# A three-part fused kernel: spreading products moved behind a slot's last cosine step, one scale moved behind two conversions, bank copies moved ahead of the rounding of pieces

## The chip, the cores and the metric

The kernel runs on one core of one Trainium2 chip, in one launch. The metric is device time in microseconds (us) of that launch. The kernel before took 914.43 us, the median of three executions (906.65, 914.43 and 920.22).

The engines are named as the profile names them: PE (TensorE, matmuls; PEld is its loading of weights), DVE (VectorE), ACT (ScalarE), POOL (GpSimd) and SP (SyncE, which issues the DMAs).

## The reference

Three stages follow each other, all in float32. `q`, `k`, `v` have the shape (4, 8, 576, 64).

```python
attn_out = attention(q, k, v)          # softmax; heads 0-3 see a window of 32, heads 4-7 every 32nd position
x = attn_out.transpose(0, 2, 1, 3).reshape(2304, 512)

h = x @ moe_w_in                       # 512 -> 2048
x = (h * cos(h)) @ moe_w_out           # 2048 -> 512

g = x @ moe2_w_gate                    # 512 -> 1536
silu = g * (1.0 / (1.0 + exp(-g)))
out = (silu * (x @ moe2_w_val)) @ moe2_w_out   # 1536 -> 512
```

## The kernel before, in words

**Number format.** A float32 product is made of three float16 products: each operand is split into a high and a low float16 part (`hi_part` on ACT, L245; `lo_part` on DVE, L248), and `mm3` (L540 to L543) adds hi·hi, hi·lo and lo·hi. So that the parts stay in range, every matrix and every block of activations is first multiplied by a power of two. That scale needs the largest magnitude of the whole matrix, over all 128 partitions, and it comes in two steps:

- *tops*, `spread_tops` (L117 to L131): DVE reduces the column maxima to one per partition, keeps the exponent and writes it on the diagonal of a 128x128 tile, `tops`.
- the *spreading product*, `common_scale` (L133 to L138): PE multiplies a matrix of ones with that tile into a bank of PSUM (L136), so that every partition sees all 128 maxima, and DVE reduces them to `q` (L137) and derives the scale and its inverse (L112 to L114).

So a scale goes DVE, then PE, then DVE. On PE the product is one matmul of 128 columns, but PE takes its work in order, and so does DVE: until `tops` is written, everything behind the product on PE stands still, and until the product is done, everything behind `q` on DVE does.

**The first MLP** (about 112 to 519 us) runs over 5 blocks of tokens (512, 512, 512, 384, 384) and 16 strips of 128 hidden columns: 80 *slots*, numbered through. The order within a slot is written out in the loop at L1009 to L1046. In slot k

- PE makes the strip, `up1(k)`: 12 matmuls into one of four banks. Then it does `down1` for one or two older strips (12 matmuls each into the accumulators).
- ACT does `up1_a(k)` (L574, rounding of the phase) and, for an older strip, `finish` (L588, the high part of its result, whose low part POOL makes, L589); later `up1_c(k-1)` (the sine, L581).
- DVE does `up1_b(k-1)` (L577), then *first-half fill*, then `up1_d(k-2)` (L584, the last step of the cosine: it multiplies by the strip that is still in the bank, and by that frees the bank), then *second-half fill*.

The four banks are handed round: a strip's bank is free again when its `up1_d` has run. A spreading product takes a bank of the same four and gives it back when `q` has read it. DVE runs behind PE in this loop, in places by more than ten microseconds, and the banks limit by how much.

**Fill** is the conversion of the later weights (`w_out`, then `gate` and `val` of the second MLP, then `w_out2`): integer steps that make float32 out of the float64 words (ACT L224, DVE L231 and L235), sums on POOL (L894), hi and lo parts, and scans for the maximum (L174). It is a queue of steps with costs, and `pump` takes from it while a credit, fed by each slot in proportion to its PE time times `SHARE` or `SHARE2`, lasts. *Urgent* pieces (`scale_pieces`: four maxima L521, tops, spreading product; `split_pieces`; `fold_pieces`) prepare the activations of the next block; `pump_urgent` takes exactly one per slot, just behind `up1_b`. Both queues can hand out a spreading product in the first half, ahead of `up1_d`.

`open_weights` (L930) queues the second MLP's weights: gate's scale, six pairs of gate (each a `half_later`, with the scans of val beside it), tops of val, val's scale, six pairs of val.

**The second MLP** (about 519 us to the end) has 30 slots s, 6 per block, in the loop from L1160. A pair of strips of gate and val is made by seven products of half the size (`multiply`, numbers 0 to 6) into banks. Sums of banks are formed by copying one bank to SBUF (`snap`, ACT L1184) and adding it to another on DVE (`join`, L1188). Then come the tanh (`gate_tanh`, ACT L652), the two steps of the silu (DVE L658 and L659), and the splitting of the result and of sums of its quarters into pieces (`piece_hi`, ACT L663; `piece_lo`, DVE L666) which the down products (`downs`, L693) take. The silu of a slot's second half, its sums and the pieces of it (`second_set`, `third_set`) are done at the start of the next slot, beside that slot's products.

## Time and profile before

| | |
|---|---|
| runs | 906.65, 914.43, 920.22 us; median 914.43 |
| the profiled execution | 906.64 us, of which 904.6 us are the span from first to last instruction |
| PE busy | 858.6 us (95%) |
| DVE busy | 688.8 us (76%) |
| ACT busy | 522.0 us (58%) |
| POOL busy | 200.0 us (22%) |
| mean granted clock of PE | 0.983 of full |
| chain that ended last | PE 68%, DVE 13%, ACT 6%, issue 5%, DMA 5%, POOL 2% |

Busy time is a share of the whole span, over parts that are limited by different engines. A wait of PE is shown behind the instruction that waited, in brackets: how long PE had been idle, and which instruction's end let it go. The window view gives the busy microseconds of each engine in a stretch, with the number of instructions, the granted clock of PE as a share of full speed, and the DMA's share.

### The profile page before, as it was taken

The numbers are of one execution on the slowest core, as the hardware profiler recorded it, in microseconds if no ns is written. First come the engines' busy times: TensorE is split into PE (matmuls) and PEld (weight loads), VectorE is DVE, ScalarE is ACT, GpSimd is POOL, SyncE is SP. The second block draws the span as 40 slices with busy tenths as digits, with TensorE's granted clock in tenths as the row PEclk, the third lists the DMA queues.
The fourth block names the chain that finished last, engine by engine and source line by source line (L and its number), as shares of the span: only waits on it lengthen the run. The fifth ranks groups of instructions, "written<-read, shape, count | busy, mean of one in ns | idle before, by whom it ended". The sixth has DMA issues, their size and how long they took to land.

```text
span 904.6 us, 18561 instructions
## 1 busy us (share of the span) xinstructions
PE 858.6 (95%) x7228; PEld 606.8 (67%) x7228; DVE 688.8 (76%) x1337; ACT 522.0 (58%) x1046; POOL 200.0 (22%) x253
## 2 busy tenths in 40 slices
PE   7999999989985989989999988999999999999998
PEld 4766644434432434445656676888888899999998
DVE  4898899894998697857977488867885776776672
ACT  4889978653665566547778455545445444544440
POOL 3444224121554365223222300000000000000000
PEclk7899999999998989999999999999999999999999
DMA  9998841565697265702514623867677688888894
GB/s 300 354 305 259 275 139 47 175 214 197 233 312 253 93 226 174 283 27 76 184 65 179 249 91 154 310 204 271 230 264 260 214 272 288 294 292 310 317 326 153
DMA packets 55912, 200.61 MB, mean 222 GB/s; under 512 B 5552, under 2 KB 19376, under 8 KB 51984
## 3 DMA queue, kind: packets, MB, share of 16 engines
q1 hardware_dynamic: 55824, 199.42, 64.6%
q8 instruction: 57, 0.93, 0.4%
q14 instruction: 31, 0.25, 0.1%
HBM read 175.41 MB, written 23.99 MB: 220 GB/s over the span
## 4 chain that ended last, share of the span: by engine, by line
PE 68%; DVE 13%; ACT 6%; issue 5%; DMA 5%; POOL 2%; SPq 0%; ACTq 0%; POOLq 0%; DVEq 0%
PE acc L693 14%; PE bank L541 11%; PE bank L542 10%; PE bank L543 10%; PE acc L541 6%; PE acc L543 6%; PE acc L542 6%; DMA vl<-v_l 3%; DVE arena L248 2%; PE bank L435 2%; PE po L488 2%; DMA v_pair<-v_s 1%; DVE tb L577 1%; DVE cv L235 1%; DVE tb L584 1%
## 5 line engine op out<-in xcount | busy, mean ns | idle before, releaser
L541 PE MATMUL bank<-xs,wi 128*128 128x256 f16 (+3 forms) x780 | 234.3, 300 | 18.3 <-DVE q L137 8.3
L542 PE MATMUL bank<-xs,wi 128*128 128x256 f16 (+3 forms) x780 | 234.3, 300 | 0.0
L543 PE MATMUL bank<-xs,wi 128*128 128x256 f16 (+3 forms) x780 | 234.1, 300 | 0.0
L589 POOL TENSOR_TENSOR arena<-tb,arena 128x512 f16<-128x512 f32 (+1 forms) x80 | 92.7, 1160 | 251.5 <-ACT arena L588 225.7
L542 PEld LDWEIGHTS <-wi 128*128 128x128 f16 x880 | 86.3, 98 | 58.5 <-issue 26.3
L541 PEld LDWEIGHTS <-wi 128*128 128x128 f16 x880 | 86.3, 98 | 46.3 <-issue 12.2
L541 PE MATMUL acc<-arena 128*128 128x512 f16 (+1 forms) x320 | 114.6, 358 | 0.0
L542 PE MATMUL acc<-arena 128*128 128x512 f16 (+1 forms) x320 | 114.5, 358 | 0.0
L543 PE MATMUL acc<-arena 128*128 128x512 f16 (+1 forms) x320 | 114.5, 358 | 0.0
L543 PEld LDWEIGHTS <-wi 128*128 128x128 f16 x880 | 86.4, 98 | 35.9 <-issue 1.9
L693 PEld LDWEIGHTS <-arena 128*128 128x128 f16 x1080 | 100.8, 98 | 8.1
L678 POOL TENSOR_TENSOR wi<-tb 128x256 f32<-128x256 f32 (+1 forms) x30 | 20.2, 672 | 347.2 <-DVE tb L659 347.2
L663 ACT ACTIVATE arena<-tb 128x256 f16<-128x256 f32 (+3 forms) x59 | 28.9, 489 | 114.0 <-DVE tb L659 109.0
L542 PEld LDWEIGHTS <-arena 128*128 128x128 f16 x600 | 58.7, 98 | 38.1 <-issue 5.6
L693 PE MATMUL acc<-arena 128*128 128x256 f16 (+1 forms) x702 | 82.0, 265 | 0.0
L543 PEld LDWEIGHTS <-arena 128*128 128x128 f16 x600 | 58.7, 98 | 32.8
L541 PEld LDWEIGHTS <-arena 128*128 128x128 f16 x600 | 58.8, 98 | 32.7 <-issue 0.3
L574 ACT ACTIVATE tb<-bank,quarter,c 128x512 int32<-128x512 f32 (+1 forms) x75 | 54.3, 723 | 41.3 <-PE bank L543 28.6
L658 DVE SCALAR_TENSOR_TENSOR tb<-tb,arena 128x512 f32<-128x512 f32 (+1 forms) x60 | 38.0, 633 | 45.0 <-ACT tb L652 45.0
L588 ACT ACTIVATE arena<-tb 128x512 f16<-128x512 f32 (+1 forms) x80 | 46.5, 582 | 39.5 <-PE acc L543 37.2
L541 PE MATMUL bank<-xs,arena 128*128 128x256 f16 (+1 forms) x240 | 62.8, 262 | 4.4 <-ACT cv L1184 3.8
L543 PE MATMUL bank<-xs,arena 128*128 128x256 f16 (+1 forms) x240 | 62.9, 262 | 0.0
(146 smaller groups left out, 1723.5 us busy)
## 6 DMA issues: line engine op xcount, KB each, us to landing
wi<-w SPq DMA_DIRECT2D x20, 1792.0 KB, 8.7
arena<-w SPq DMA_DIRECT2D x60, 576.0 KB, 4.4
raw<-w_out SPq DMA_DIRECT2D x56, 512.0 KB, 4.8
arena<-w SPq DMA_DIRECT2D x10, 1792.0 KB, 14.9
raw<-w_gate SPq DMA_DIRECT2D x24, 512.0 KB, 4.3
raw<-w_val SPq DMA_DIRECT2D x24, 512.0 KB
w<-arena SPq DMA_DIRECT2D x36, 256.0 KB, 3.2
raw<-w_in SPq DMA_DIRECT2D x16, 512.0 KB
```

Of the source, the lines that this page charges most:

```text
L248: nc.vector.scalar_tensor_tensor(out=dst, in0=src, scalar=s, in1=hi, op0=ALU.mult, op1=ALU.subtract)
L435: nc.tensor.matmul(out=self.sc[r, i, :], lhsT=qk_t[self.i][r, q0:q0 + 64], rhs=qk_t[self.i][r, k0:k0 + w], start=i == 0, stop=False)
L541: nc.tensor.matmul(out=o, lhsT=w[:, 0, c], rhs=x[0], start=first, stop=False, **kw)
L542: nc.tensor.matmul(out=o, lhsT=w[:, 0, c], rhs=x[1], start=False, stop=False, **kw)
L543: nc.tensor.matmul(out=o, lhsT=w[:, 1, c], rhs=x[0], start=False, stop=last, **kw)
L574: nc.scalar.activation(out=c["w"].bitcast(I32), in_=c["ph"], func=AF.Identity, scale=turn[c["blk"]], bias=quarter)
L588: nc.scalar.activation(out=g[:, 0, 0:n], in_=w, func=AF.Copy)
L589: nc.gpsimd.tensor_tensor(out=g[:, 1, 0:n], in0=w, in1=g[:, 0, 0:n], op=ALU.subtract)
L658: nc.vector.scalar_tensor_tensor(out=t, in0=t, scalar=1.0, in1=gate, op0=ALU.add, op1=ALU.mult)
L663: nc.scalar.activation(out=to, in_=src, func=AF.Copy, scale=2.0 ** -11)
L678: nc.gpsimd.tensor_tensor(out=t_sums[:, 0, 0:h], in0=c["t"][0][:, h:2 * h], in1=c["t"][0][:, 0:h], op=ALU.subtract)
L693: nc.tensor.matmul(out=o[:, c], lhsT=w[:, 256 * i + 128 * c:256 * i + 128 * c + 128], rhs=unit(u)[:, x:x + h], start=j == c == i == 0, sto ...
```

## The change

Four edits. The number of instructions on each engine is the same as before, and the order of DMA issues is too.

1. Spreading products of `scale_later` (weights) and of `scale_pieces` (activations) are marked `late`. The first half of a slot's fill stops in front of one; `pump_urgent(False)` ahead of `up1_d` takes an urgent piece only if it isn't late, and `pump_urgent(True)` behind `up1_d` takes one only if it is. As both calls stand in every slot, tops and spreading product of an urgent chain now fall into one slot where they took two.
2. val's scale is queued behind the first two conversions of val's first pair (`ready`), where it stood directly behind tops.
3. In the second MLP `snap(px)` stands ahead of the last slot's tanh and silu, and the two halves of `second_set` stand behind the second and third snaps, just ahead of `third_set`.
4. `SHARE2` is 0.78 where it was 0.75 (blocks 2 to 4).

```diff
-SHARE, SHARE2, SB = 0.95, 0.75, 2
+SHARE, SHARE2, SB = 0.95, 0.78, 2
...
-        def pump(share):
+        late = set()
+
+        def pump(share, spread=True):
             credit[0] = min(credit[0] + share, max(share, 1.0))
-            while fill and credit[0] > 0:
+            while fill and credit[0] > 0 and (spread or fill[0][1] not in late):
                 step_fill()
...
         def scale_later(mat, bound):
-            later(0.6, lambda: scale_w.__setitem__(mat, common_scale(tops[mat], bound)))
+            def spread():
+                scale_w[mat] = common_scale(tops[mat], bound)
+            late.add(spread)
+            later(0.6, spread)
...
-            yield 0.6, lambda: scales.__setitem__(blk, common_scale(box["top"], TX))
+            def spread():
+                scales[blk] = common_scale(box["top"], TX)
+            late.add(spread)
+            yield 0.6, spread
...
-        def half_later(j, mi, mat, beside=None):
+        def half_later(j, mi, mat, beside=None, ready=None):
...
+            if ready:
+                begin([])
+                ready()
             parts = [[(0, lambda q=q: hi(q)), (0.7, lambda q=q: lo(q))] for q in range(3)]
...
                 top_later("val")
-                scale_later("val", TW_IN)
                 for j in range(NPR):
-                    half_later(j, 1, "val")
+                    half_later(j, 1, "val", ready=None if j else lambda: scale_later("val", TW_IN))
...
-        def pump_urgent():
-            if urgent:
+        def pump_urgent(now=None):
+            if urgent and (now is None or (urgent[0][1] in late) == now):
...
-                pump_urgent()
-                pump(budget * 0.5)
+                pump_urgent(False)
+                pump(budget * 0.5, False)
                 up1_c(steps[-1][2])
                 if len(steps) > 1:
                     up1_d(steps[-2][2])
+                pump_urgent(True)
                 pump(budget * 0.5)
...
+            a = snap(px)
             if last:
                 t = gate_tanh(last, 1)
                 silu(last, 1, t)
-            a = snap(px)
...
             if last:
                 piece_sums(last)
-                his, los = second_set(last)
-                run(his)
             pz = halves(bank(), h)
             multiply(4, w, x, pz, h, True)
             b = snap(pz)
...
-            if last:
-                run(los)
             pump_urgent()
             multiply(5, w, x, px, h, False)
             a = snap(px)
             if last:
+                his, los = second_set(last)
+                run(his)
+                run(los)
                 his, los = third_set(last)
                 run(his)
```

**DVE, slots 39 and 40 of the first MLP** (the scale of block 1's result for the second MLP; L577 is `up1_b`, L584 `up1_d`, L248, L231 and L235 are fill). Before, from the tops to the scale:

```order
L130 TENSOR_SCALAR tops<-id_76,p 128x128
L248 SCALAR_TENSOR_TENSOR arena<-arena,s_3646 128x512
L231 TENSOR_SCALAR arena<-arena 128x512
L235 SCALAR_TENSOR_TENSOR arena<-raw,arena 128x512
L584 SCALAR_TENSOR_TENSOR tb<-tb,bank 128x512
L248 SCALAR_TENSOR_TENSOR arena<-arena,s_3646 128x512 x2
L248 SCALAR_TENSOR_TENSOR arena<-arena,s_3646 128x256
L231 TENSOR_SCALAR arena<-arena 128x512
L235 SCALAR_TENSOR_TENSOR arena<-raw,arena 128x512
L577 SCALAR_TENSOR_TENSOR tb<-bank,c_3439,tb 128x512
L137 TENSOR_REDUCE q<-bank 128x1
L112 RECIPROCAL s_3982<-q 128x1
```

Now, one slot earlier (L586 is `up1_b`, L593 `up1_d`, L250 and L233 are L248 and L231):

```order
L130 TENSOR_SCALAR tops<-id_76,p 128x128
L250 SCALAR_TENSOR_TENSOR arena<-arena,s_3694 128x512
L250 SCALAR_TENSOR_TENSOR arena<-arena,s_3694 128x256
L593 SCALAR_TENSOR_TENSOR tb<-tb,bank 128x512
L137 TENSOR_REDUCE q<-bank 128x1
L112 RECIPROCAL s_3877<-q 128x1
L113 TENSOR_SCALAR inv_3878<-q 128x1
L114 TENSOR_SCALAR s_3877<-s_3877 128x1
L233 TENSOR_SCALAR arena<-arena 128x512
L237 SCALAR_TENSOR_TENSOR arena<-raw,arena 128x512
L586 SCALAR_TENSOR_TENSOR tb<-bank,c_3437,tb 128x512
```

`q` stood behind the next slot's `up1_b`; now it stands behind the `up1_d` of the slot that wrote tops, with two fill steps between tops and `up1_d`.

**DVE, slots 34 and 35** (tops and scale of val). Before:

```order
L130 TENSOR_SCALAR tops<-id_76,p 128x128
L137 TENSOR_REDUCE q<-bank 128x1
L112 RECIPROCAL s_3646<-q 128x1
L113 TENSOR_SCALAR inv_3647<-q 128x1
L114 TENSOR_SCALAR s_3646<-s_3646 128x1
L577 SCALAR_TENSOR_TENSOR tb<-bank,c_3439,tb 128x512
L521 TENSOR_REDUCE parts_3_3561<-xy_69 128x1
```

Now:

```order
L130 TENSOR_SCALAR tops<-id_76,p 128x128
L233 TENSOR_SCALAR arena<-arena 128x512
L586 SCALAR_TENSOR_TENSOR tb<-bank,c_3437,tb 128x512
L526 TENSOR_REDUCE parts_3_3570<-xy_69 128x1
L237 SCALAR_TENSOR_TENSOR arena<-raw,arena 128x512
L233 TENSOR_SCALAR arena<-arena 128x512
L593 SCALAR_TENSOR_TENSOR tb<-tb,bank 128x512
L237 SCALAR_TENSOR_TENSOR arena<-raw,arena 128x512
L137 TENSOR_REDUCE q<-bank 128x1
```

On PE val's product stood behind slot 34's down products, with that of `ys` just ahead of it; now it stands behind those of slot 35, and the two conversions of val's first pair (L233 and L237, twice) stand ahead of `q`.

**ACT, a slot of the second MLP** (L1242 is the last copy of the slot before). Before:

```order
L1242 ACTIVATE arena<-bank 128x2x256
L652 ACTIVATE tb<-arena,c_5641 128x512
L1184 ACTIVATE cv<-bank 128x512
L663 ACTIVATE arena<-tb 128x2x256
L1184 ACTIVATE cv<-bank 128x512 x2
L663 ACTIVATE arena<-wi 128x4x256
```

Now (L1253 is that copy, L1196 `snap`, L661 the tanh, L672 `piece_hi`):

```order
L1253 ACTIVATE arena<-bank 128x2x256
L1196 ACTIVATE cv<-bank 128x512
L661 ACTIVATE tb<-arena,c_5657 128x512
L1196 ACTIVATE cv<-bank 128x512 x2
L672 ACTIVATE arena<-tb 128x2x256
L672 ACTIVATE arena<-wi 128x4x256
```

The first copy goes ahead of the tanh, and the rounding of `second_set` from between the first and second copy to behind the third.

## Rows read from the trace of the kernel before

**Rows 1.** The page: busy time of the engines.

```profile
PE 858.6 (95%) x7228; PEld 606.8 (67%) x7228; DVE 688.8 (76%) x1337; ACT 522.0 (58%) x1046; POOL 200.0 (22%) x253
```

**Rows 2.** The waits view: engine, tile, line waited for: us, times, longest.

```profile
DVE q L137 <- PE bank L136: 19.9, 7, 5.8
...
PE bank L136 <- DVE tops L130: 10.0, 3, 8.7
PE bank L541 <- DVE q L137: 8.3, 7, 3.4
PE bank L541 <- DVE tb L584: 7.6, 6, 2.3
PE bank L541 <- ACT cv L1184: 5.3, 8, 1.5
```

**Rows 3.** Windows: us busy (instructions) of PE, PEld, DVE, ACT, POOL; clock, DMA, GB/s.

```profile
190.00:200.00 10.00, 8.49 (x40) 3.81 (x39) 9.48 (x19) 6.91 (x11) 2.50 (x3) 1.00 0.76 240
...
290.00:300.00 10.00, 7.06 (x26) 2.92 (x26) 4.54 (x14) 1.68 (x3) 0.00 (x0) 0.68 0.24 84
...
330.00:340.00 10.00, 5.96 (x18) 2.12 (x17) 9.61 (x19) 7.32 (x12) 6.80 (x7) 0.69 0.69 229
```

**Rows 4.** PE's timeline, slots 33 to 36: start, us, instruction, [idle before it].

```profile
270.50 0.38 PE L541 MATMUL bank<-xs,wi 128*128 128x512 f16 x1
270.72 0.38 PE L542 MATMUL bank<-xs,wi 128*128 128x512 f16 x1
...
292.94 0.27 PE L136 MATMUL bank<-tops,ones 128*128 128x128 bf16 x1 [8.73 <-DVE tops L130]
...
299.82 0.38 PE L541 MATMUL bank<-xs,wi 128*128 128x512 f16 x1
```

**Rows 5.** DVE's timeline, slots 32 to 36.

```profile
275.50 0.67 DVE L584 SCALAR_TENSOR_TENSOR tb<-tb,bank 128x512 f32<-128x512 f32 x1
...
292.63 0.25 DVE L130 TENSOR_SCALAR tops<-id,p 128x128 bf16<-128x128 bf16 x1
...
301.24 0.94 DVE L231 TENSOR_SCALAR arena<-arena 128x512 int32<-128x512 int32 x1 [6.20 <-ACT arena L224]
```

**Rows 6.** ACT's and POOL's timeline ahead of val's tops.

```profile
284.66 0.63 ACT L588 ACTIVATE arena<-tb 128x512 f16<-128x512 f32 x1
...
286.48 3.45 POOL L894 TENSOR_TENSOR arena<-arena 128x256 f32<-128x256 f32 x4
```

**Rows 7.** PE's and DVE's timeline, slots 38 to 41.

```profile
318.09 0.38 PE L541 MATMUL bank<-xs,wi 128*128 128x512 f16 x1
...
322.22 0.74 DVE L577 SCALAR_TENSOR_TENSOR tb<-bank,c,tb 128x512 f32<-128x512 f32 x1
...
324.00 0.68 DVE L584 SCALAR_TENSOR_TENSOR tb<-tb,bank 128x512 f32<-128x512 f32 x1
...
331.81 0.22 PE L136 MATMUL bank<-tops,ones 128*128 128x128 bf16 x1 [0.61 <-DVE tb L584]
335.46 0.58 PE L541 MATMUL bank<-xs,wi 128*128 128x512 f16 x1 [3.43 <-DVE q L137]
...
340.53 0.46 PE L541 MATMUL acc<-arena 128*128 128x512 f16 x1
```

**Rows 8.** PE's timeline, two later slots with a wait for a scale.

```profile
399.76 0.32 PE L541 MATMUL bank<-xs,wi 128*128 128x384 f16 x1 [1.97 <-DVE q L137]
...
464.36 0.32 PE L541 MATMUL bank<-xs,wi 128*128 128x384 f16 x1 [1.38 <-DVE q L137]
```

**Rows 9.** Windows of the second MLP, columns as in Rows 3.

```profile
540.00:550.00 10.00, 6.57 (x58) 5.44 (x56) 7.56 (x14) 5.10 (x10) 0.73 (x1) 1.00 0.51 185
...
590.00:600.00 10.00, 10.00 (x94) 8.97 (x92) 5.16 (x8) 3.81 (x7) 0.73 (x1) 1.00 0.53 151
```

**Rows 10.** ACT's timeline at the start of a slot of the second MLP.

```profile
543.83 0.72 ACT L652 ACTIVATE tb<-arena,c 128x512 f32<-128x512 f32 x1
...
546.04 0.63 ACT L663 ACTIVATE arena<-tb 128x512 f16<-128x512 f32 x1 [1.00 <-DVE tb L659]
```

## The prediction

> **What bounds the kernel now.** I read the page first: PE is busy for 95% of the span and DVE for 76% [rows 1], so as a whole it is bound by PE, and what a change can give is PE's idle time. The waits of PE come next [rows 2]: after the attention part few lines hold it up. A spreading product waits for its tops (10.0 us, of which one wait is 8.7), strips wait for a bank that `q` holds (8.3 in seven waits, the longest 3.4), for a bank that `up1_d` holds (7.6 in six), and products of the second MLP for a copied bank (5.3 in eight). DVE's own wait for spreading products (19.9 us in seven) counts only where PE ends up waiting behind it.
>
> Then the windows [rows 3], to see which engine sets the pace where these waits lie. In the first MLP between 190 and 340 us DVE is 9.5 to 9.6 of 10 us busy while PE has gaps: there DVE sets the pace and the ring of four banks passes it on to PE. From 590 us on PE is 10.00 of 10 us busy [rows 9], and nothing that the change does there can move the end. In the same windows the granted clock tells a second cost: 1.00 in 190 to 200 us, where the waits are of 2.3 us and less, but 0.68 and 0.69 around the 8.73 us wait and around the pair 0.61 and 3.43 us [rows 3, 4, 7]. It fell to its lower level (1.2 of 2.4 GHz) there and came back. From 335.46 to 340.53 one strip's 12 matmuls took 5.07 us [rows 7]; at full clock they start 0.216 us apart (two are shown rounded, 270.50 and 270.72 [rows 4]), so a strip of 512 tokens or a down product of one takes 2.6: 2.5 us lost. The other place, with nearly the same mean clock, I put at 2.0.
>
> **What goes.** `q` no longer stands in front of an `up1_d`, and its product has been on PE for two fill steps and that `up1_d` when DVE comes to it. So the seven waits on `q` can go: 3.43 [rows 7], 1.97 and 1.38 [rows 8], and four that share the remaining 1.52. With them go the 0.61 [rows 7], val's 8.73 [rows 4], the last scale's share of the tops waits (0.7 of 10.0, estimated as half of what lies beside the 8.73 in three waits), and both drops of the clock, 4.5. That is 8.3 + 0.6 + 8.7 + 0.7 + 4.5 = 22.8 us, 2.5% of the profiled 906.6, if nothing comes in their place.
>
> **What comes.** Before, PE met a spreading product a slot after DVE had been told to write its tops. Now both belong to one slot, so PE stands at the product until DVE, which is behind, comes to that slot's tops; and the next strip needs the bank of the `up1_d` that lies behind the first half of that slot's fill. Where DVE runs late this is a new stall. Three places:
>
> - *Slot 32* (scale of block 0's result). PE began strip 33 at 270.50 [rows 4]. Its bank now comes from the `up1_d` of slot 32, which DVE ended at 275.50 + 0.67 = 276.2 [rows 5]: 5.7 us later.
> - *Slot 35* (val). PE now does strip 35 and a down product (2.6 + 2.6 us) before it asks for the tops, so of 8.73 some 3.5 are left. But the tops hang on a chain from PE: ACT L588 behind slot 34's down products (284.66), POOL's sums (3.45 us), ACT's and DVE's parts, tops at 292.63 + 0.25, 8.7 us behind PE's last matmul at 284.2 [rows 4 to 6]. The stall in slot 32 shifts that start by about 4.7 us (5.7 less what the next strips waited for their banks). Tops then end near 297.6, PE is there at 294.4 (strip 33 from 276.2, its down product, then strips and down products of slots 34 and 35: 276.2 + 5.2 + 7.8 + 5.2), and strip 36 waits another 3 us for its `up1_d`. That is 300.5, and it was 299.82 [rows 4]. Val's gain is given back by the stall that slot 32 has got.
> - *Slot 38* (scale of block 1's result). PE began strip 39 at 318.09 [rows 7]. DVE came to that slot's `up1_b` at 322.22 and to its `up1_d` at 324.00; with the tops between them (0.25 for the last of three steps at 292.63 [rows 5], the other two put at as much each) `up1_d` ends near 324.68 + 0.75 = 325.4. Strip 39 begins 7.3 us later. Then slot 39 (2.6 + 5.2), slot 40 (2.6 + 2.6) and strip 41 (2.6) end at 341.0 at full clock; strip 41 ended at 340.53 before [rows 7].
>
> So this stretch comes out 0.5 us later at full clock. Two things move it. DVE had idled 6.20 us at 301.24, for val's first conversions, which stood behind the scale and behind ACT [rows 5]; these conversions now stand ahead of the scale, so DVE can gain 0 to 6.2, and I take 2, nearer to nothing, as PE and ACT bring what it works on. And the clock: the three new stalls are about 6, 6 and 7 us in two parts each, and resemble the pair that halved it (0.61 and 3.43). Between none and three drops of 2.5 us the cost is 0 to 7.5; since DVE, not PE, sets the pace there and a slow strip is hidden behind its lag, I take 2. Term: +0.5 − 2 + 2 = **+0.5**.
>
> The Trainium skill, in "TensorE: Matmul & The Clock Gate", section "HAM oscillation — how this bites in real kernels", says that waits between bursts of matmuls drop the clock, so that the next burst starts cold, each time. The trace agrees for the two long waits (clock 0.68 and 0.69) and shows none for the short ones (1.00 in 190 to 200 us). Taken strictly, all three new stalls pay.
>
> *Blocks of 384 tokens* (slots 48 to 79): 1.97, 1.38, two of the four small waits (0.8) and the 0.7 go, 4.9 in all. Three spreading products with their tops in the same slot come (slots 54, 64 and 77). DVE is less far behind here; each costs between 0 and 3.4 (the longest wait on `q`), I take 1.4, near what these slots show now [rows 8]. Term: −4.9 + 4.2 = **−0.7**.
>
> *The second MLP.* The first copy goes ahead of a tanh of 0.72, the second ahead of a rounding of 0.63 [rows 10]; the eight waits of 5.3 us [rows 2] lie in the first ten slots, where PE is 6.6 of 10 us busy in the worst window [rows 9]. All could go: −5.3. But the circle from tanh over silu, join and the last copy back to tanh sets the pace in these slots, and a copy, put at the 0.63 of the rounding, is now part of it: in slots 1 to 5 that is up to 5 × 0.63 = +3.1. Pieces come later for the downs, which from 590 us have slack. I take −1.5, between the two and somewhat on the side of the shown waits. Term: **−1.5**.
>
> *Slot 9 and `SHARE2`*: the early product may meet its tops late (0 to 1.3 by the two smaller waits on tops); DVE limits the slots that follow, so 0. A share of 0.78 moves fill earlier and adds no instruction: 0, with its ends within those of the first term. No DMA issue changes place, so SP's queue and POOL's order stay.
>
> **Sum:** +0.5 − 0.7 − 1.5 = −1.7 us on the profiled 906.6 (904.6 of span and 2.0 around it), which is also the fastest of the three runs. The median lies 7.8 above it; the forecast is set against the median: 914.4 − 1.7, **913**.
>
> **Rivals.**
>
> - *A, the waits change places* (forecast): 905 to 921, taking the ends of the terms but not all at once, and 4 us for a median of three runs that lie 13.6 apart. Chance 0.62.
> - *B, what comes is cheap.* DVE uses its idle 6.2 us fully, is then less far behind when PE reaches slots 35 and 38, and the clock does not fall. For it: DVE's idle time lies just ahead of these slots. Against it: 9.6 of 10 us busy right there. Between half and all of 22.8 us: 892 to 904. Chance 0.23.
> - *C, slower: the clock falls at each of the three new stalls and DVE's lag hides none of it.* It decides where DVE is more than about the down product's 5 us behind PE when the slot's tops are asked for, so that each stall becomes as long as the 8.73 one. +7.5 in place of +2, no gain of DVE's idle time (+2), second MLP +3.1 in place of −1.5: 913 + 5.5 + 2 + 4.6 = 925. Chance 0.10. The rule of the Trainium skill's "TensorE: Matmul & The Clock Gate" that is told above, followed strictly, is this rival.
> - *D, nothing of it reaches the end:* the ring of banks and DVE's total work set 190 to 340 us whatever the order: 914, give or take the 4 us. Chance 0.05.
>
> **Numbers.** 80% range: A and D whole, the upper part of B, the lower part of C: 899 to 922. A measurement of this kernel tells about 2% (18 us) from no change. Faster by more needs 896 or less: a third of B, 0.07. Slower by more needs 933: the worst of C, 0.02. Else 0.91.
>
> **What would show it.** If I am right, the waits on `q` are nearly gone from PE's list, those on tops and on `up1_d` have grown to some 20 us or more, with stalls at the strips behind slots 32, 35 and 38, and the second MLP begins within 3 us of when it did. If B is right, waits on tops stay under 5 us and the granted clock keeps 1.00 between 280 and 350 us. If C is right, three windows of the first MLP show a clock of 0.7 or less. My slot 38 fails first if DVE gets there earlier than 322 us, and the term of the second MLP if waits for copied banks stay at 5 us.

## The result and the profile after

The changed kernel takes 917.36 us (median of 22 executions, 913.97 to 932.36), the kernel before 909.59 (22 executions, 906.35 to 920.22). The ratio is 1.0075, with a 95% interval from 1.0054 to 1.0096: about 7 us **slower**. The ratio leaves out executions in a slower state of the chip (three of the 22, 928 us and more), so it is not the quotient of the two medians. The forecast was no change, 1.7 us less than before. The time itself, 917, lies inside the forecast range of 899 to 922, which was set around a median of three executions (914.43) that came out 4.8 above that of 22; the direction is what the forecast had wrong.

The two profiled executions differ by more, 904.6 and 919.0 us of span. Strip 1 of the first MLP (the second one; strip 0 is made inside the attention part) starts 6.77 us later in the one of after, and up to there the kernels have the same instructions: in all sixteen profiles of this study, all with the same attention part, that start lies anywhere from 112.9 to 122.5 us. So I count from that strip on, and in two parts: the *first MLP*, from the start of strip 1 to the start of strip 79, and the *rest*, from there to the end of the span. Before they took 390.47 and 401.25 us, now 399.57 and 399.77: **+9.1 and −1.5**. That is the 7 to 8 us that the medians show.

PE's waits after the change (engine, tile, line waited for: us, times, longest; L593 is `up1_d`, L1196 the copy of a bank), which answer to [rows 2]:

```profile
PE bank L550 <- DVE tb L593: 18.1, 13, 2.8
PE bank L136 <- DVE tops L130: 13.4, 6, 5.4
...
PE bank L550 <- ACT cv L1196: 4.0, 2, 2.7
PE bank L550 <- DVE arena L1200: 1.3, 4, 0.3
```

The waits on `q`, 8.3 us before, are gone. Those on tops went from 10.0 to 13.4 and those on `up1_d` from 7.6 to 18.1. PE's timeline shows where (start, us, instruction, [idle before]; the L136 rows are spreading products, the L550 rows the strips behind them or with a wait of their own):

```profile
144.41 0.22 PE L136 MATMUL bank<-tops,ones 128*128 128x128 bf16 x1 [1.23 <-DVE tops L130]
155.96 0.38 PE L550 MATMUL bank<-xs,wi 128*128 128x512 f16 x1 [0.97 <-DVE tb L593]
279.37 0.22 PE L136 MATMUL bank<-tops,ones 128*128 128x128 bf16 x1 [1.68 <-DVE tops L130]
282.21 0.58 PE L550 MATMUL bank<-xs,wi 128*128 128x512 f16 x1 [2.63 <-DVE tb L593]
306.07 0.22 PE L136 MATMUL bank<-tops,ones 128*128 128x128 bf16 x1 [2.71 <-DVE tops L130]
309.08 0.58 PE L550 MATMUL bank<-xs,wi 128*128 128x512 f16 x1 [2.79 <-DVE tb L593]
334.19 0.27 PE L136 MATMUL bank<-tops,ones 128*128 128x128 bf16 x1 [5.43 <-DVE tops L130]
335.84 0.59 PE L550 MATMUL bank<-xs,wi 128*128 128x512 f16 x1 [1.39 <-DVE tb L593]
352.04 0.38 PE L550 MATMUL bank<-xs,wi 128*128 128x512 f16 x1 [1.43 <-DVE tb L593]
422.77 0.22 PE L136 MATMUL bank<-tops,ones 128*128 128x128 bf16 x1 [1.72 <-DVE tops L130]
423.84 0.32 PE L550 MATMUL bank<-xs,wi 128*128 128x384 f16 x1 [0.85 <-DVE tb L593]
```

These are slots 9 and 14, 32 and 33, 35 and 36, 38 and 39, 41, 54 and 55. The late products of slots 32, 35, 38 and 54 make PE wait twice: for the tops, and at the next strip for `up1_d`. DVE's timeline of slot 38 has both causes in one place:

```profile
332.85 0.74 DVE L586 SCALAR_TENSOR_TENSOR tb<-bank,c,tb 128x512 f32<-128x512 f32 x1
...
333.88 0.25 DVE L130 TENSOR_SCALAR tops<-id,p 128x128 bf16<-128x128 bf16 x1
334.05 1.14 DVE L250 SCALAR_TENSOR_TENSOR arena<-arena,s 128x512 f16<-128x512 f32 x2
335.11 0.68 DVE L593 SCALAR_TENSOR_TENSOR tb<-tb,bank 128x512 f32<-128x512 f32 x1
335.70 0.28 DVE L137 TENSOR_REDUCE q<-bank 128x1 f32<-128x128 f32 x1
```

PE stood from 328.8 to 334.19, until the tops were there, and then until `up1_d` ended at 335.8, behind two fill steps. The windows (us busy of PE, PEld, DVE, ACT, POOL; clock) show the granted clock fall behind four of the five places:

```profile
285.00:295.00 10.00, 10.00 (x41) 4.17 (x40) 7.16 (x13) 4.89 (x8) 2.19 (x3) 0.85 0.75 245
...
305.00:315.00 10.00, 6.14 (x23) 2.46 (x23) 6.19 (x18) 2.81 (x5) 4.01 (x5) 0.83 0.46 150
...
335.00:345.00 10.00, 9.16 (x35) 3.79 (x35) 3.71 (x10) 0.79 (x2) 0.00 (x0) 0.79 0.36 119
...
425.00:435.00 10.00, 10.00 (x54) 5.66 (x53) 7.84 (x15) 5.93 (x11) 1.73 (x2) 0.85 0.23 75
```

In PE's timeline the lower clock shows as matmuls that start 0.42 to 0.43 us apart instead of 0.216, here in strip 33:

```profile
282.60 0.63 PE L551 MATMUL bank<-xs,wi 128*128 128x512 f16 x1
283.02 0.63 PE L552 MATMUL bank<-xs,wi 128*128 128x512 f16 x1
```

Added up over PE's timeline from strip 1 to strip 79, PE's idle time grew from 25.4 to 31.0 us, and what matmuls lost by starting further apart than at full clock grew from 6.0 to 10.0 (this second sum is worked out from the starts of all matmuls). So of the +9.1 us some 5.6 are waits and some 4 are the clock; shorter pauses gave back half a microsecond. Three of the four drops lie in the stretch for which the forecast allowed 2 us: strip 34 starts 7.3 us later than before where strip 33 started 4.9 later, strip 37 3.9 where strip 36 was at 2.5, and strip 40 12.6 where strip 39 was at 11.0. Behind slot 54 it is 11.2 at strip 56 where it was 9.5 at strip 55. That is not one profile's chance: val_a_slot_later, the same program up to slot 34, lost 3.6 us to the clock in slots 32 and 33 (strip 34 starts 8.4 us late).

The first of them was not hidden. The chain to val's tops starts from PE's down products of slot 34 and goes over ACT and POOL; DVE stands idle for it:

```profile
298.22 0.63 ACT L597 ACTIVATE arena<-tb 128x512 f16<-128x512 f32 x1 [4.34 <-PE acc L552]
302.36 1.25 DVE L250 SCALAR_TENSOR_TENSOR arena<-arena,s 128x512 f16<-128x512 f32 x1 [6.66 <-ACT arena L247]
305.76 0.26 DVE L130 TENSOR_SCALAR tops<-id,p 128x128 bf16<-128x128 bf16 x1
```

Counted from strip 1 the chain started 6.8 us later than before (298.22 less 6.77, against 284.66 [rows 6]).

### The profile page after: what moved, and what is told of

It is laid out like the page before. It is cut to its first block, busy times and chain, and to the rows that moved or that the text cites. A ratio compares the mean times of both kernels' runs of the same rounds, so it can differ in the third digit from the quotient of the medians.

```text
span 919.0 us, 18508 instructions
## 1 busy us (share of the span) xinstructions
PE 867.0 (94%) x7228; PEld 611.6 (67%) x7228; DVE 687.6 (75%) x1337; ACT 520.5 (57%) x1046; POOL 196.4 (21%) x253
## 4 chain that ended last, share of the span: by engine, by line
PE 64%; DVE 14%; issue 7%; DMA 6%; ACT 4%; POOL 4%; SPq 0%; POOLq 0%; ACTq 0%; DVEq 0%
PE acc L702 13%; PE bank L550 10%; PE bank L552 10%; PE bank L551 10%; PE acc L550 5%; PE acc L552 5%; PE acc L551 5%; POOL arena L903 2%; PE bank L440 2%; PE po L493 2%; DVE arena L250 2%; DMA vl<-v_l 1%; DVE tb L593 1%; DVE cv L237 1%; DVE tb L586 1%
## 5 line engine op out<-in xcount | busy, mean ns | idle before, releaser
L550 PE MATMUL bank<-xs,wi 128*128 128x256 f16 (+3 forms) x780 | 235.6, 302 | 22.9 <-DVE tb L593 18.1
L598 POOL TENSOR_TENSOR arena<-tb,arena 128x512 f16<-128x512 f32 (+1 forms) x80 | 90.6, 1133 | 259.2 <-ACT arena L597 229.8
L550 PEld LDWEIGHTS <-wi 128*128 128x128 f16 x880 | 86.6, 98 | 50.2 <-issue 16.5
L550 PE MATMUL acc<-arena 128*128 128x512 f16 (+1 forms) x320 | 115.0, 359 | 0.0
L550 PEld LDWEIGHTS <-arena 128*128 128x128 f16 x600 | 59.1, 98 | 33.3 <-issue 0.8
L672 ACT ACTIVATE arena<-tb 128x256 f16<-128x256 f32 (+3 forms) x59 | 28.6, 485 | 87.5 <-DVE tb L668 87.5
L1196 ACT ACTIVATE cv<-bank 128x512 f32<-128x512 f32 (+1 forms) x90 | 49.6, 552 | 35.7 <-PE bank L552 35.5
L550 PE MATMUL bank<-xs,arena 128*128 128x256 f16 (+1 forms) x240 | 63.3, 264 | 0.7 <-DVE arena L1200 0.7
```

The lines of the kernel that those rows point to most:

```text
L550: nc.tensor.matmul(out=o, lhsT=w[:, 0, c], rhs=x[0], start=first, stop=False, **kw)
L598: nc.gpsimd.tensor_tensor(out=g[:, 1, 0:n], in0=w, in1=g[:, 0, 0:n], op=ALU.subtract)
L672: nc.scalar.activation(out=to, in_=src, func=AF.Copy, scale=2.0 ** -11)
L1196: nc.scalar.activation(out=t, in_=src, func=AF.Copy)
```

## The experiments

Ratios are against the kernel before on the same chip, with 95% intervals. The last two columns are the two parts of the profiled execution, from the starts of strips 1 and 79 in PE's timeline; before the first was 390.47 and the second 401.25.

How far these two columns can be trusted shows where kernels share a part. The rest repeats to 0.1 us: 401.23 to 401.29 in five kernels whose second MLP is that of before and whose tops and late product don't share a slot, 402.23 to 402.30 in four that have edit 3 besides. The first MLP repeats less well: before and only_mlp2 have the same one and took 390.47 and 391.88; without_late, val_and_share and val_share_pieces share another and took 385.24, 384.76 and 386.85. Differences of some 2 us in that column tell nothing by themselves.

| kernel | median us | ratio | first MLP | rest |
|---|---|---|---|---|
| changed kernel | 917.36 | 1.0075 [1.0054, 1.0096] | 399.57 | 399.77 |
| only_late | 912.07 | 1.0017 [0.9988, 1.0046] | 396.70 | 399.01 |
| only_val | 906.15 | 0.9966 [0.9940, 0.9992] | 387.13 | 401.27 |
| only_mlp2 | 910.59 | 1.0023 [0.9991, 1.0054] | 391.88 | 402.23 |
| only_share | 906.22 | 0.9980 [0.9950, 1.0010] | 387.58 | 401.29 |
| without_late | 904.80 | 0.9945 [0.9915, 0.9975] | 385.24 | 402.30 |
| without_val | 921.11 | 1.0125 [1.0069, 1.0181] | 403.15 | 399.71 |
| without_share | 907.57 | 0.9964 [0.9934, 0.9994] | 391.38 | 399.68 |
| val_and_share | 903.74 | 0.9950 [0.9916, 0.9984] | 384.76 | 401.23 |
| late_two_slots | 915.67 | 1.0063 [1.0030, 1.0095] | 396.50 | 402.29 |
| late_fill_behind | 912.00 | 1.0032 [1.0007, 1.0057] | 394.35 | 399.75 |
| two_slots_fill_behind | 906.51 | 0.9963 [0.9943, 0.9983] | 385.85 | 402.25 |
| val_a_slot_later | 915.23 | 1.0067 [1.0038, 1.0095] | 398.33 | 399.71 |
| val_share_pieces | 904.03 | 0.9934 [0.9908, 0.9960] | 386.85 | 401.43 |
| two_slots_old_mlp2 | 906.36 | 0.9969 [0.9942, 0.9996] | 386.79 | 401.24 |

**The four edits, each alone** on the kernel before. Their diffs are the parts of the change.

Late products (edit 1, only_late):

> The kernel before with the first edit alone (spreading products late, tops and product in one slot); val's scale, the second MLP and the share stay as they were. Theory W (PE waits for tops written in the same slot, and for the up1_d behind them): strips lag the kernel before by about 2 us from slot 14 on (slot 9's product waits for its tops), by 4 to 5 us more behind slot 32, by some 6 more behind slot 38 or 39, and part is given back where waits on q go; the time is 5 to 10 us over that of before (ratio 1.005 to 1.011). Theory V (val's move is what costs): within 2 us of before. Theory S (the larger share): within 2 us of before.

In the trace the first MLP is 6.2 us longer and the rest 2.2 shorter (the chains of urgent pieces are a slot shorter, and the last scale no longer falls into the second MLP); the timed ratio doesn't tell it from before. The places are the ones that were expected: against before, strip 14 starts 2.5 us later, strip 33 5.3, strip 39 10.3.

Val's move (edit 2, only_val):

> The kernel before with the second edit alone (val's scale behind its first two conversions). Theory W: without the stall in slot 32 that moves the chain ahead of val's tops, PE's 8.73 us wait shrinks to about 3.5 and the drop of the clock behind it goes; 3 to 7 us faster than before (ratio 0.992 to 0.997). Theory V: the conversions ahead of the scale hold up DVE in the stretch in which it sets the pace; 3 to 8 us slower.

Faster by 3.1 us (0.7 to 5.5 by the interval), as theory W has it; theory V falls. The way there is only half that of theory W: in place of the one wait PE stood 2.35 us for the tops and 2.79 at the next strip for `up1_d`, and the clock fell all the same (0.83 in 305 to 315 us).

The second MLP (edit 3, only_mlp2):

> The kernel before with the third edit alone (copies of banks ahead of the rounding of pieces in the second MLP). By the traces of before and after the second MLP, from its first product to the end, is 1.5 us shorter, so 1 to 2 us faster (ratio 0.998 to 0.999), with the gain before 600 us. A rival: the copy in the circle of tanh, silu and join costs more than the waits it saves, and the gain belongs to the different state in which the first MLP ended; then 0 to 3 us slower.

The rest is 1.0 us *longer*, the rival's case. The −1.5 us that the changed kernel shows there is late products' −2.2 and this edit's cost.

The share (edit 4, only_share):

> The kernel before with the fourth edit alone (SHARE2 0.78 for 0.75). Theory W: no instruction is added, the fill only comes a little earlier; within 2 us of before. Theory S (DVE's first halves grow by 4% in slots 32 and on, where DVE sets the pace, and up1_d and tops come later): 3 to 8 us slower.

By the trace 2.9 us less in the first MLP; the timed interval holds 1, so the gain is not shown. So no edit alone costs more than 4 us in its trace, and the ratios of the four add up to 0.1% less than before, where all four together cost 7. Two or more of them must work against each other.

**Leaving out one.** Without late products (without_late):

```diff
-                pump_urgent(False)
-                pump(budget * 0.5, False)
+                pump_urgent()
+                pump(budget * 0.5)
...
-                pump_urgent(True)
```

> The changed kernel without its first edit: val's move, the second MLP's order and the share of 0.78 together, products handed out as before. If the edits add up (val 3.1 us faster, the second MLP 2.1 slower, the share 1.8 faster, by the fast runs of the single edits): 905 to 909, 2 to 4 us under before, and 8 to 11 under the changed kernel. If the changed kernel's extra cost sits in val's move beside the larger share: over before, 912 or more.

The first case, and clearly: 0.9945. Late products cost 14.3 us in the first MLP beside the other edits (399.57 against 385.24), 6.2 alone.

Without val's move (without_val):

```diff
                 top_later("val")
+                scale_later("val", TW_IN)
                 for j in range(NPR):
-                    half_later(j, 1, "val", ready=None if j else lambda: scale_later("val", TW_IN))
+                    half_later(j, 1, "val")
```

> The changed kernel without its second edit: late products, the second MLP's order and the share, with val's product directly behind its tops. If late products alone cost 1.6 us and the changed kernel's remaining 6 come from late products beside val's move (val's conversions ahead of its scale delay up1_d and tops of slot 38): 910 to 913. If val's move helps here as it did alone: 919 to 921.

Val's move helps beside late products too (first MLP 403.15 without it). It isn't what they collide with. Late products and the share together cost 12.7 us in the first MLP, where alone they were 6.2 and −2.9. The timed ratios say the same: 1.0125 with edits 1, 3 and 4 together, where the three alone add up to 1.0020.

Val's move and the share, nothing else (val_and_share):

> The kernel before with val's move and the share of 0.78, no late products and the second MLP as before: the two edits that were faster alone. If they add up: 904 to 906, 4 to 6 us under before (ratio 0.993 to 0.996). If both shorten the same wait (val's 8.73 us): 906 to 908, as either alone.

They add up: 384.76 us is 5.7 less, by parts 3.3 and 2.9, and the time, 903.74, lies in the first range but for 0.3 us.

**What makes late products dear.** Tops a slot ahead of the product, which stays behind `up1_d` (late_two_slots):

```diff
+                ripe = urgent and urgent[0][1] in late
                 pump_urgent(False)
...
-                pump_urgent(True)
+                if ripe:
+                    pump_urgent(True)
```

> The changed kernel, but an urgent spreading product is handed out behind up1_d only if its tops were written in an earlier slot (as before), so the chain of urgent pieces takes its old number of slots. Theory W (the wait for tops written in the same slot costs): PE finds the tops ready behind slots 23, 34 and 40; the waits on tops fall from 13.4 us to about that of val alone, 3 us, and the time comes 5 to 9 us under that of the changed kernel (908 to 912). Theory B (what costs is that the strip behind a spreading product takes the bank of an up1_d, behind the first half of the fill, where it took the bank of q, directly behind up1_b): these waits stay, the time is within 3 us of the changed kernel.

Between the two, and by its time (915.67) in theory B's range. The first MLP gives back 3.1 us (the timed ratios, 1.0063 and 1.0075, do not tell the two kernels apart) and no wait on tops of 0.3 us or more is left in it, but the waits on `up1_d` grew:

```profile
PE bank L550 <- DVE tb L593: 23.5, 8, 6.7
```

PE's timeline around slot 40 of this kernel:

```profile
341.28 0.22 PE L136 MATMUL bank<-tops,ones 128*128 128x128 bf16 x1 [1.97 <-DVE tb L593]
...
347.93 0.58 PE L550 MATMUL bank<-xs,wi 128*128 128x512 f16 x1 [6.43 <-DVE tb L593]
```

and DVE's, from `up1_b` (L586) of that slot:

```profile
343.26 0.75 DVE L586 SCALAR_TENSOR_TENSOR tb<-bank,c,tb 128x512 f32<-128x512 f32 x1
344.06 0.96 DVE L233 TENSOR_SCALAR arena<-arena 128x512 int32<-128x512 int32 x1
345.05 1.10 DVE L237 SCALAR_TENSOR_TENSOR arena<-raw,arena 128x512 int32<-128x512 int32 x1
346.07 1.21 DVE L250 SCALAR_TENSOR_TENSOR arena<-arena,s 128x512 f16<-128x512 f32 x1
347.20 0.67 DVE L593 SCALAR_TENSOR_TENSOR tb<-tb,bank 128x512 f32<-128x512 f32 x1
347.80 0.28 DVE L137 TENSOR_REDUCE q<-bank 128x1 f32<-128x128 f32 x1
```

The strip got its bank from `up1_d` at 347.87, behind three fill steps. Before, `q` stood directly behind `up1_b`, and the strip took the product's own bank back from it, after 3.43 us [rows 7]. So the change moved the release of a bank behind the first half of the fill.

The longest wait, 6.67 us, is at strip 35, and there the fill in front of `up1_d` (which ended at 300.08) was itself waiting for ACT (a row of PE and one of DVE):

```profile
300.13 0.59 PE L550 MATMUL bank<-xs,wi 128*128 128x512 f16 x1 [6.67 <-DVE tb L593]
...
297.58 1.90 DVE L250 SCALAR_TENSOR_TENSOR arena<-arena,s 128x512 f16<-128x512 f32 x2 [4.54 <-ACT arena L247]
```

A fill step ahead of the release costs not only its own time but also what it waits for.

The same with no fill ahead of `up1_d` in the product's slot (two_slots_fill_behind):

```diff
-                pump(budget * 0.5, False)
+                if not ripe:
+                    pump(budget * 0.5, False)
...
-                pump(budget * 0.5)
+                pump(budget * (1.0 if ripe else 0.5))
```

> As the kernel with tops a slot ahead of the late product, and in the product's slot the whole fill behind up1_d and the product. Theory W with B: neither tops nor fill stand ahead of the bank; the wait of 6.7 us behind slot 40 falls to 2 to 4, and the first MLP from 396.5 us to 390 to 393; time 908 to 912. Rival L: within 1.5 us of the kernel with tops a slot ahead (915.7).

More than was expected: the first MLP takes 385.85 us, and late products cost nothing any more beside val's move and the share (384.76 to 386.85 without them). The same place on PE and on DVE:

```profile
334.68 0.22 PE L136 MATMUL bank<-tops,ones 128*128 128x128 bf16 x1 [1.96 <-DVE tb L593]
338.06 0.58 PE L550 MATMUL bank<-xs,wi 128*128 128x512 f16 x1 [3.16 <-DVE tb L593]
```

```profile
336.67 0.74 DVE L586 SCALAR_TENSOR_TENSOR tb<-bank,c,tb 128x512 f32<-128x512 f32 x1
337.33 0.68 DVE L593 SCALAR_TENSOR_TENSOR tb<-tb,bank 128x512 f32<-128x512 f32 x1
```

The product waits as long as there (1.96 and 1.97), the strip 3.16 us where it was 6.43. The 3.27 us between them are the three fill steps, 0.96 + 1.10 + 1.21.

Fill behind `up1_d` in the slots of tops and product, but both in one slot as in the changed kernel (late_fill_behind):

```diff
+                hold = any(u[1] in late for u in list(urgent)[:2])
                 pump_urgent(False)
-                pump(budget * 0.5, False)
+                if not hold:
+                    pump(budget * 0.5, False)
...
-                pump(budget * 0.5)
+                pump(budget * (1.0 if hold else 0.5))
```

> The changed kernel, but in a slot that holds the tops or the product of an urgent chain the whole fill is done behind up1_d and the product: no fill between up1_b and up1_d there. Theory B: the stalls behind slots 32, 38 and 54 lose the time of the fill steps of a first half (some 1 to 4 us each), tops no more than before; first MLP 392 to 397 us where the changed kernel had 399.6, time 910 to 914. Rival L (DVE is just late; fill not done now is done a slot later ahead of the next up1_d): within 1.5 us of the changed kernel.

The waits on tops stay, 13.4 us as in the changed kernel, those on `up1_d` fall from 18.1 to 12.8, and the first MLP by 5.2. So in the profiled first MLP, against the changed kernel, taking away the tops' wait gives 3.1 us, taking away the fill 5.2, and both 13.7; by the timed ratios it is 1.1, 3.9 and 10.2. The clock is in these numbers: with the fill behind, the drop at strip 33 did not come (strip 34 starts 2.3 us later than before, not 7.3), and no run takes the clock away by itself.

**The share.** Back at 0.75 in the changed kernel (without_share):

> The changed kernel with SHARE2 back at 0.75. By the traces the first MLP (strip 1 to strip 79) took 390.5 us before, 396.7 with late products alone, 403.2 with late products and the larger share, 399.6 with all edits. Theory B (a larger first half stands ahead of the up1_d for whose bank the next strip waits): the share costs beside late products what it gained alone; first MLP 392 to 395 us, time 910 to 913, 4 to 7 us under the changed kernel. Rival N (share adds up as alone, 3 us faster): first MLP 401 to 403, time 919 to 921.

8.2 us less in the first MLP, and 907.57 us, more gain than theory B's range; rival N falls. In the strips' starts the difference to the changed kernel opens from strip 34 on (2.1 us there, 8.0 at strip 36, 4.7 at strip 53), where val's product falls into slot 36 instead of 35, two slots behind its tops, and once more behind slot 54 (8.7 at strip 56). To see whether val's slot is what does it (val_a_slot_later):

```diff
                 begin([])
+                later(1.0, lambda: None)
                 ready()
```

> The changed kernel with an empty fill step of cost 1.0 ahead of val's scale, so that its product goes from slot 35 to slot 36, two slots behind its tops, as it does with SHARE2 at 0.75; the share stays 0.78. Theory P (the larger share costs beside late products because the credit then lets val's product fall into the slot right behind its tops): the waits of 2.71 and 2.79 us behind slot 35 go, strips 36 and 37 stand 4 to 8 us earlier, the first MLP takes 391 to 395 us instead of 399.6; time 909 to 913. Rival B2 (the larger share costs because every first half ahead of an up1_d has grown): strips 36 to 41 as in the changed kernel within 2 us, first MLP 397 to 400.

Mostly not. Strips 36 and 37 come 3.7 and 3.1 us sooner, but then the product of slot 38 waits 6.0 and 2.49 us, and the first MLP ends only 1.2 us shorter, which is within the scatter of that column. That is the rival's range at the end, though not its strips.

**The rest of it.** Of the third edit only the rounding behind the third copy, beside val's move and the share (val_share_pieces):

```diff
-                his, los = second_set(last)
-                run(his)
...
             a = snap(px)
             if last:
+                his, los = second_set(last)
+                run(his)
+                run(los)
                 his, los = third_set(last)
```

> The kernel before with val's move and the share of 0.78, and of the third edit only that second_set is rounded behind the third copy; the first copy stays behind tanh and silu. By the traces the time from strip 79 to the end was 401.2 us in kernels with the old order and 402.3 with the whole third edit. If the copy ahead of the tanh is what costs (it lies in the circle that sets the pace in slots 2 to 6): 399 to 401 us here, time 902 to 904. If the later pieces cost: 402 to 403, time 904 to 905.

The rest takes 401.43 us where the old order had 401.23 and the whole edit 402.30: of its 1.0 us, 0.2 comes with the later rounding and 0.8 with the copy ahead of the tanh. The expected 399 to 401 was too hopeful: the rounding alone gains nothing. Profiles carry these two numbers (the column repeats to 0.1 us), the timed intervals don't.

Late products without their costs and the second MLP in its old order (two_slots_old_mlp2: the two-slot kernel with its fill behind, edit 3 undone):

> The kernel with tops a slot ahead and the fill behind, and the second MLP in its old order: late products, val's move and the larger share without what was found to cost. By the traces the first MLP takes 386 us and the rest 401.2 in place of 402.2: 904 to 906, 1 us under the kernel with the third edit (906.5) and 3 to 6 us under before, no better than val's move and the share alone (903.7).

906.36, just above the expected range, under before and not under val's move with the share alone. Late products gain nothing over handing products out ahead of `up1_d`. The lowest ratios of all are those of the three kernels with val's move and the larger share and without late products, 0.9934 to 0.9950; they beat both kernels, and the intervals don't tell them apart.

## Why the prediction was wrong, point by point

- **What goes: right.** The seven waits on `q` and val's wait of 8.73 us are gone. What comes also had the right places: slots 32, 35 and 38, and in the later blocks 54; and the waits on tops and `up1_d`, 31.5 us together, are the "some 20 us or more". The three new stalls took 4.3, 5.5 and 6.8 us in two parts each, where "about 6, 6 and 7" were forecast. What did not come true is that the second MLP begins within 3 us of when it did: strip 79 starts 9.1 us later.
- **Slot 32: right in size.** Strip 33 starts 4.9 us later than before, counted from strip 1; 5.7 were forecast.
- **The step that failed is the term of this stretch, "+0.5 − 2 + 2", by its clock first.** Three drops of the clock could "cost 0 to 7.5", and 2 were taken "since DVE, not PE, sets the pace there and a slow strip is hidden behind its lag". That rested on a reading that the rows do not bear: DVE is not 9.5 to 9.6 of 10 us busy all through 190 to 340 us; between 290 and 300 it is 4.54 [rows 3]. Val's tops hang on a chain that starts from PE, as the text itself said of slot 35, and what PE lost at the lower clock in strip 33 came out at strip 36. From strip 31 to strip 46 PE lost 7.2 us at the lower clock, where it had lost 4.8 before. With the 4.5 that were to go and the 2 that were allowed, a gain of 2.5 was forecast; 2.4 more were lost, so 4.9 of the miss are the clock. PE's idle time there grew from 14.7 to 21.3 us, some 6.6, where 3.0 were in the sum (0.5 and 4.5, less the 2 of DVE's idle time). Together the stretch cost 9.2 us; the sum had +0.5.
- **Slot 38 shows how it ran on.** I took DVE's time at that slot over from the trace of before (322.22). Counted from strip 1 DVE reached it 3.9 us later (332.85 less 6.77 is 326.1), since strips 36 to 38 were already 2.5 to 3.9 us late, not 0.7. Most of that is the clock: the chain to val's tops started 6.8 us late instead of the forecast 4.7, and strip 36 lost another 1.4. So strip 39 was 11.0 us late instead of 7.3. Strip 40 then lost another 1.7 at the lower clock, and strips 41 and 43 stood once more for an `up1_d` (1.43 and 1.05).
- **DVE's 6.2 us of idle time: hoped for, not seen.** I took 2 us of gain for val's conversions moved ahead of the scale. DVE stood idle just as long in the changed kernel, 6.66 us at 302.36, ahead of val's tops: it waited for PE's chain. Val's move as a whole does gain, 3.3 us in the first MLP alone and 3.6 beside late products (403.15 without it), but by the long wait of PE that it shortens.
- **Where the clock fell.** It fell behind slots 32, 35, 38 and 54. The rule of the Trainium skill's "TensorE: Matmul & The Clock Gate", in "HAM oscillation — how this bites in real kernels", that waits between bursts drop the clock, held here at the late products of four slots that PE had to wait for, and not at that of slot 9 (1.23 and 0.97 us, four strips apart).
- **`SHARE2` at nothing: wrong.** "Moves fill earlier and adds no instruction: 0." Alone it gains 2.9 us in the profiled first MLP, beside late products it costs 8.2 (10 by the timed ratios): what it moves earlier stands in first halves, ahead of the `up1_d` that now frees the bank. That this is how it costs is argued, not shown. That it costs nothing once tops and fill are out of the way (385.85 us) is shown; through which of the first halves it acts is open, as val's slot explained only 1.2 us of it.
- **Blocks of 384 tokens: −0.7 forecast, −0.1 measured** (9.2 us at strip 48, 9.1 at strip 79): 2.7 and 2.2 us came back with the waits on `q`, and slot 54 took 4.6 with its clock.
- **The second MLP: right number, wrong reason.** −1.5 forecast and measured, but that is luck: edit 3 costs 1.0 alone, and late products gain 2.2, for which the forecast had at most the 0.7 of the last scale, in another term. My own argument, that a copy is now part of the circle, was the better one (0.8 of the 1.0 came with the copy ahead of the tanh), and the eight waits that I set against it turned into others (the waits on the join and two of 1.3 and 2.7 on copies).
- **Slot 9 at nothing: right in the end.** Strips 14 to 23 start 2.2 to 2.5 us later; by strip 31 that was made up, by the waits on `q` that went and by DVE's pace.

Of the rivals it is C, "slower", at about three quarters of its price (+7.8 between the medians, where it had +10.6 on 914.4). It was right that the clock falls at each of the three stalls, that the lag does not hide it (7.2 us, where it had 7.5) and that DVE's idle time gains nothing; it was wrong on the second MLP (+3.1, measured −1.5), the stalls stayed shorter than the 8.73 us that it named, and its sign, windows with a clock of 0.7 or less, did not come (0.79 at the lowest in those shown). The drops come behind the waits, and no run separates the two: that moving the release of the bank behind the fill costs is shown, by the kernels that take fill and tops out of the way; how much of it goes by the clock is an estimate from the profiles.

## What to carry to other kernels

In a ring of buffers the place in an engine's order where a buffer is *given back* matters as much as where work waits: before moving a consumer behind something, ask which buffer the next producer takes then, and what stands ahead of its release. A round trip over two engines wants its halves a stage apart, and no work that could wait in front of the release, least of all work that itself waits for another engine; here either alone gave 3 and 5 us in the profiles, both together 14 (1, 4 and 10 by the timed ratios). And don't carry an engine's times over from the old trace behind the first new stall: move them by the stalls already added, or the second and third come out too cheap. Before a loss on one engine is called hidden behind another, check which engine starts the chain that the next wait hangs on.

## What was not expected of the hardware

The attention part, the same instructions in all kernels here, ended up to 9.6 us apart in single profiles (strip 1 from 112.88 to 122.50 us), while from strip 2 to strip 30 the kernels with the same program there agree to within 0.1 us. A difference of two profiles is worth little until it is counted from the first point after such a part. Behind strip 30 the same program still came out up to 2.1 us apart.

The same wait can leave the granted clock up or drop it. Behind slot 54 it fell after waits of 1.72 and 0.85 us one matmul and some 0.2 us apart (0.85 in 425 to 435 us). At strip 21 PE waits 2.3 us in all sixteen profiles. In seven of them the clock stayed up there (in before 1.00 from 185 to 200 us, with a further wait of 1.5 us at the next strip, [rows 3] in part). In the other nine it fell, here in only_val:

```profile
198.00:208.00 10.00, 10.00 (x39) 4.22 (x39) 9.55 (x17) 6.26 (x11) 2.32 (x2) 0.83 0.76 247
```

In those nine the next strip starts at the same time as in the others, 6.85 us after strip 21, and its wait of 1.5 us is gone: there the slow matmuls only filled a wait. So a single profile that shows 1.00 behind a wait does not show that such a wait is safe.
